# Scores masked by VectorE, no GpSimd arithmetic in the first layer, and only TensorE in source order

## The chip, the core and the metric

The kernel runs on one core of a Trainium2 chip. The metric is device time in microseconds (us) of one execution. The engines named here are TensorE (PE; its weight loads are PEld), VectorE (DVE), ScalarE (ACT), GpSimd (POOL) and SyncE (SP), whose queue issues most of the transfers. Each engine runs its own instructions in the order in which the program gives them.

## What is computed

```python
# gated linear attention: 4 sequences, 8 heads, 768 steps, head dimension 48
for t in range(S):
    state = alpha[:, :, t, :, None] * state + np.einsum('bhd,bhe->bhde', k[:, :, t], v[:, :, t])
    y[:, :, t] = np.einsum('bhd,bhde->bhe', q[:, :, t], state)
# first layer: 3072 tokens of 384, 2048 hidden; g = max(h, 0) squared
h = x @ w_in
r = np.maximum(h, 0.0)
x = (r * r) @ w_out
# second layer: each token goes to one of 8 experts of 1024 hidden
logits = x @ w_gate + modality_bias[modality_id]
e_idx = np.argmax(logits, axis=1)
out[mask] = gate_w[mask, None] * (np.maximum(x[mask] @ w1[e], 0.0) @ w2[e])
```

Inputs w_in and w_out arrive as 64-bit numbers; the kernel turns them into 32-bit ones itself.

## The kernel before

The 3072 tokens are 24 attention units of 128 tokens (unit u) and 12 blocks of 256 tokens (block n, two units each). For a unit, `a_scan` and `a_scan2` make running products of alpha (VectorE's scans, lines 319 and 331) and multiply k and q by them (lines 320 and 332: on VectorE for units 0 and 1, on GpSimd after that, by `MULD`). `a_p` makes the 128x128 scores (line 341); ScalarE copies them out of PSUM (line 348) and GpSimd sets those on the wrong side of the diagonal to zero (line 349). `a_y` multiplies them with v (lines 389 and 392), ScalarE copies y (line 394), and y goes to memory (line 397; issued from ScalarE's queue for units below `PRE` = 4, from SP's after that). `a_state` adds the unit to the running state (line 377). `a_yload` reads a block's x back (line 401) and `a_x` splits it into a high and a low part, xh and xl (lines 407 and 408).

Every product of the layers is made as three matmuls of such parts (`mm3`, line 430). A block's first layer is 16 steps; step (n, f) makes h for 128 hidden columns (tile ph), then g = max(h, 0) squared (ScalarE's line 981 and VectorE's line 985), its parts gh (ScalarE, line 989) and gl (line 991: VectorE, or GpSimd for block 1, by `POOLGL`), and three steps later adds to the output (tile po). Blocks 0 and 1 run interleaved, block 1 eight steps behind, while the weights are made ready. For each of the 16 weight blocks f, `convert(f)` decodes two halves (mag on ScalarE, line 275; three integer operations on VectorE, lines 278 to 280) and splits them (wh on ScalarE, line 258; wl on GpSimd, line 259). `gate_flip` transposes the second half (line 298, copied by line 300), and `gate_columns` appends eight columns to it (lines 305 to 307; line 307 is VectorE's). Tile st holds four loaded pieces, and the next load is issued when a piece is used up.

`put` places attention units, routing and the checks of alpha's range (`a_check`) at steps of the first layer. From step g0+9 of the last block the second layer's first weights are loaded and split (`m_load`, `m_w`). The block `with tc.manual_schedule(engines={...})` names the engines that keep the order of the source; the instructions of other engines are put in order when the program is built, by when it reckons their operands ready.

Of the kernel before, what the change touches and what calls it, by code (L numbers as in the profile page):

```python
# [8 lines left out]
F32 = mybir.dt.float32  # L9
F32R = mybir.dt.float32r  # L10
BF16 = mybir.dt.bfloat16
I32 = mybir.dt.int32
AF = mybir.ActivationFunctionType
ALU = mybir.AluOpType
# [9 lines left out]
C = 128  # L24
NU = N // C
CPB = S // C
HP = H // 2
HR = 112
TB = 256
# [150 lines left out]
def gla_moe_moe2(ctx: ExitStack, tc: tile.TileContext, ain, vin, al_d, wio_d, wg_d, wgt_d, mid_d, mb_d, w12_d, out):  # L180
    nc = tc.nc
    pe, act, dve, pool, sp = nc.tensor, nc.scalar, nc.vector, nc.gpsimd, nc.sync

    def mkpool(name, bufs=1, **kw):
        return stack.enter_context(tc.tile_pool(name=name, bufs=bufs, **kw))

    stack = ctx
    const = mkpool("const")
# [4 lines left out]
    p1 = mkpool("p1", 1)  # L193
# [10 lines left out]
    yt_d = dram.tile([DM, N], F32, name="yt_d")  # L204

    ident = const.tile([128, 128], F32, name="ident")
    tri = const.tile([128, 128], BF16, name="tri")
    ones = const.tile([128, 128], BF16, name="ones")
    iota = const.tile([128, NCOL], F32, name="iota")
    tok1 = const.tile([128, NU], F32, name="tok1")  # L210
# [44 lines left out]
    def split(t, lo_eng=dve):  # L255
        hi = wpool.tile([128, 2 * DM + E], F32R, name="wh")
        lo = wpool.tile([128, 2 * DM + E], F32R, name="wl")
        act.copy(out=hi[:, 0:2 * DM], in_=t)  # L258
        lo_eng.tensor_tensor(out=lo[:, 0:2 * DM], in0=t, in1=hi[:, 0:2 * DM], op=ALU.subtract)  # L259
        return (hi[:, 0:DM], lo[:, 0:DM]), (hi[:, DM:], lo[:, DM:])  # L260

    wreg = {}

    def load_w(f):
        for k in range(2):
            stage(("w", f, k), wio_d[f, :, DM * k:DM * (k + 1)].bitcast(I32))

    def convert(f):

        w = rows_p.tile([128, 2 * DM], I32, tag="row", name="w")  # L270
        for k in range(2):
            raw = wst.pop(("w", f, k)).bitcast(I32).rearrange("p (n two) -> p n two", two=2)
            half = w[:, DM * k:DM * (k + 1)]
            mag = p3.tile([128, DM], F32, name="mag")
            act.activation(out=mag, in_=raw[:, :, 1].bitcast(F32), func=AF.Copy, scale=2.0 ** -112)
            yield
            m = mag.bitcast(I32)
            dve.tensor_scalar(out=half, in0=m, scalar1=-(2 ** 31), scalar2=None, op0=ALU.bitwise_and)
            dve.scalar_tensor_tensor(out=half, in0=raw[:, :, 0], scalar=29, in1=half, op0=ALU.logical_shift_right, op1=ALU.bitwise_or)
            dve.scalar_tensor_tensor(out=half, in0=m, scalar=3, in1=half, op0=ALU.logical_shift_left, op1=ALU.bitwise_or)  # L280
            if k and f + 2 < NF:
                load_w(f + 2)
            yield
        w = w.bitcast(F32)
        wreg["w", f] = split(w, pool)
        gates.append((w[:, DM:], *wreg["w", f][1]))
        yield

# [24 lines left out]
    def a_scan(u):  # L313
# [3 lines left out]
        ar = ar3.rearrange("p g t -> p (g t)")  # L317
        mul = dve if u < MULD else pool
        dve.tensor_tensor_scan(out=ar, data0=al[:, 0:HP * (C + 1)], data1=delta.rearrange("p g t -> p (g t)"), initial=0.0, op0=ALU.mult, op1=ALU.add)  # L319
# [16 lines left out]
    def a_p(u):  # L336
        x = un[u]
        pp = [ps1.tile([128, HP, C], F32, tag=t, name="pp") if u in ATG else ps2.tile([128, HP, C], F32, tag="out" if u == 1 else "P", name="pp") for t in ("ms", "y")]
        for hp in range(HP):
            for j, (r0, r1) in enumerate(((0, 64), (64, HR))):  # L340
                pe.matmul(out=pp[j][:, hp, :], lhsT=x["k"][r0:r1, hp * C:(hp + 1) * C], rhs=x["q"][r0:r1, (HP - 1 - hp) * C:(HP - hp) * C], start=True, stop=True)
        x["pt"] = []
        for j in range(2):
            if u in (1, 3):
                pt = p3.tile([128, 2, XW], F32, tag="ob", name="pt").rearrange("p j d -> p (j d)")[:, 0:HP * C].rearrange("p (g t) -> p g t", g=HP)
            else:
                pt = p1.tile([128, HP, C], F32, tag=f"pt{j}", name="pt")
            act.copy(out=pt, in_=pp[j])  # L348
            pool.affine_select(out=pt, in_=pt, compare_op=ALU.is_ge, fill=0.0, base=-127, pattern=[[0, HP], [1, 128]], channel_multiplier=1)  # L349
            x["pt"].append(pt)  # L350

    def a_kt(u):
# [28 lines left out]
    def a_y(u):  # L381
        x = un[u]
        c = u // 2 % CPB

        py = ps1.tile([HR, HP, C], F32, tag="y", name="py")
        if c:
            for hp in range(HP):
                for r0, r1 in ((0, 64), (64, HR)):
                    pe.matmul(out=py[r0:r1, hp, :], lhsT=st_t[u % 2][r0:r1, hp, 0:r1 - r0], rhs=x["q"][r0:r1, (HP - 1 - hp) * C:(HP - hp) * C], start=not hp, stop=False, skip_group_check=True)
        for hp in range(HP):  # L390
            for j, (r0, r1) in enumerate(((0, 64), (64, HR))):
                pe.matmul(out=py[r0:r1, hp, :], lhsT=x["v"][:, hp, r0:r1], rhs=x["pt"][j][:, hp, :], start=not c and not hp, stop=True, skip_group_check=True)
        y = p1.tile([HR, HP, C], F32, name="y")
        act.copy(out=y, in_=py)
        yd = yt_d.rearrange("(g j e) t -> j e g t", g=HP, j=2)
        for j, (r0, r1) in enumerate(HRNG):
            (act if u < PRE else sp).dma_start(out=yd[j, :, :, u * C:(u + 1) * C], in_=y[r0:r1])

    def a_yload(n):
        x = p1.tile([128, ND, TB], F32, name="xf")  # L400
        (act if n < 2 else sp).dma_start(out=x, in_=yt_d.rearrange("(d p) t -> p d t", p=128)[:, :, n * TB:(n + 1) * TB])
        xt[n] = x

    def a_x(n):
# [27 lines left out]
    def layer1(w, x):  # L432
        ph = ps2.tile([128, TB], F32, tag="h", name="ph")
        for d in range(ND):
            mm3(ph, w, x, (slice(None), slice(d * 128, (d + 1) * 128)), (slice(None), d), d == 0, d == ND - 1)
        return ph
# [336 lines left out]
    PRE = 4  # L773
    LEAD = 8
    LAG1 = 3
    POOLGL = (1,)
    WARM = 4
    MULD = 2

    ATG = {4: 12, 5: 18, 6: 24}  # L780
    gq = {}
# [1 line left out]
    if True:  # L783
# [15 lines left out]
        def keep_warm(n):  # L799
            warm = ps2.tile([HR, HP * C], F32, tag="h", name="warm")  # L800
            for _ in range(n):
                pe.matmul(out=warm, lhsT=delta[:, 0, 0:HR], rhs=delta.rearrange("p g t -> p (g t)")[:, 0:HP * C], start=True, stop=True)
        keep_warm(WARM)
        pool.memset(ones, 1.0)
        pool.affine_select(out=tri, in_=ones, compare_op=ALU.is_ge, fill=0.0, base=-1, pattern=[[1, 128]], channel_multiplier=-1)
        pool.memset(cum, 0.0)
# [121 lines left out]
        for n in range(2, NB):  # L928
            g0 = two + (n - 2) * NF
            for i in range(2):  # L930
                u = 2 * n + 3 + i
# [35 lines left out]

            spread([g0 + k for k in (2, 5, 7)], check())

        with tc.manual_schedule(engines={mybir.EngineType.PE, mybir.EngineType.Activation, mybir.EngineType.DVE, mybir.EngineType.Pool}):  # L970
            early()
            for gs in range(len(seq) + LAG1):
                n, f = seq[gs] if gs < len(seq) else (NB, 0)
                for step in at.get(gs, ()):
                    step()
                gate = None
                alone = gs < LEAD
                if n < NB:
                    ph = layer1(wreg["w", f][0], xt[n])
                    g = p3.tile([128, TB], F32, name="g")  # L980
                    act.activation(out=g, in_=ph, func=AF.Relu)  # L981
                    if n == 0:
                        cv(f + 1)
                        gate = gate_flip()
                    dve.scalar_tensor_tensor(out=g, in0=ph, scalar=0.0, in1=g, op0=ALU.max, op1=ALU.mult)  # L985
                    if n == 0:
                        cv(f + 2)
                    gh = gpool.tile([128, TB], F32R, name="gh")
                    act.copy(out=gh, in_=g)  # L989
                    gl = gpool.tile([128, TB], F32R, name="gl")  # L990
                    (pool if n in POOLGL else dve).tensor_tensor(out=gl, in0=g, in1=gh, op=ALU.subtract)  # L991
                    gq[n, f] = (gh, gl)
                if n == 0:
                    cv(f + 2)
                if gs >= LAG1:
                    moe1_l2(*seq[gs - LAG1])
                if n == 0 and alone:
                    cv(f + 2)
                if gate:
                    gate_columns(*gate)  # L1000
                if n == 0 and alone:
                    cv(f + 3)
                if n == 1 and gs < two:
                    cv(f + LEAD + 2)
                    cv(f + LEAD + 3)
# [111 lines left out]
```

## Time and profile before

| | |
|---|---|
| median of 3 runs | 861.3 us (860.91 to 862.28) |
| the profiled execution | 860.75 us, its span 859.0 us |
| TensorE matmuls busy | 787.2 us (92%) |
| VectorE busy | 536.0 us (62%) |
| ScalarE busy | 418.5 us (49%) |
| GpSimd busy | 192.0 us (22%) |

Busy time is the time in which an engine runs an instruction, its waiting inside one included. The granted clock is TensorE's: 1.00 is 2.4 GHz and 0.50 is 1.2 GHz, and a value between them is a mean over a stretch.

### The profile page before, as it was taken

The numbers are of one execution on the slowest core, as the hardware profiler recorded it, in microseconds if no ns is written. First come the engines' busy times: TensorE is split into PE (matmuls) and PEld (weight loads), VectorE is DVE, ScalarE is ACT, GpSimd is POOL, SyncE is SP. The second block draws the span as 40 slices with busy tenths as digits, with TensorE's granted clock in tenths as the row PEclk, the third lists the DMA queues.
The fourth block names the chain that finished last, engine by engine and source line by source line (L and its number), as shares of the span: only waits on it lengthen the run. The fifth ranks groups of instructions, "written<-read, shape, count | busy, mean of one in ns | idle before, by whom it ended". The sixth has DMA issues, their size and how long they took to land. (4 is left out here: it accounts for less than half of the span.)

```text
span 859.0 us, 16686 instructions
## 1 busy us (share of the span) xinstructions
PE 787.2 (92%) x6174; PEld 752.1 (88%) x6174; DVE 536.0 (62%) x1278; ACT 418.5 (49%) x911; POOL 192.0 (22%) x206
## 2 busy tenths in 40 slices
PE   6477697999999999999999999997999999999992
PEld 4366697999999999999999999997998999999992
DVE  7577977665656565656565656456787666666631
ACT  2344453434444445545454454442666666666641
POOL 4232453442111111111111111001112232223110
PEclk9568877999999999999999999999999999999997
DMA  9646434304121323232323210102688777777600
GB/s 261 168 126 170 122 93 127 108 30 121 54 83 55 93 69 104 73 101 79 95 82 97 64 45 25 33 17 73 208 244 275 235 227 222 224 229 226 207 30 17
DMA packets 56021, 105.40 MB, mean 123 GB/s; under 512 B 9163, under 2 KB 29141, under 8 KB 55920
## 3 DMA queue, kind: packets, MB, share of 16 engines
q1 hardware_dynamic: 50256, 92.92, 36.9%
q0 software_dynamic: 3200, 9.65, 3.4%
q10 hardware_dynamic: 2464, 1.57, 0.6%
q8 instruction: 53, 0.87, 0.5%
q14 instruction: 48, 0.39, 0.1%
HBM read 89.95 MB, written 14.36 MB: 121 GB/s over the span
## 5 line engine op out<-in xcount | busy, mean ns | idle before, releaser
L430 PE MATMUL ph<-xh,wh 128*128 128x256 f32 x864 | 251.0, 291 | 8.0 <-DVE g L985 5.2
L430 PE MATMUL ph<-xh,wl 128*128 128x256 f32 x864 | 244.9, 283 | 1.8 <-POOL wl L259 1.8
L430 PE MATMUL ph<-xl,wh 128*128 128x256 f32 x864 | 245.4, 284 | 0.4 <-DVE xl L408 0.4
L430 PE MATMUL po<-wh,gh 128*128 128x392 f32 (+1 forms) x584 | 203.9, 349 | 4.2 <-ACT ob L870 2.9
L430 PE MATMUL po<-wl,gh 128*128 128x392 f32 (+1 forms) x584 | 200.0, 342 | 0.0
L430 PE MATMUL po<-wh,gl 128*128 128x392 f32 (+1 forms) x584 | 199.9, 342 | 0.0
L430 PEld LDWEIGHTS ph<-xh,wh 128*128 128x128 f32 x864 | 165.0, 191 | 11.4 <-DVE g L985 5.9
L430 PEld LDWEIGHTS ph<-xh,wl 128*128 128x128 f32 x864 | 165.0, 191 | 2.6 <-POOL wl L259 2.6
L430 PEld LDWEIGHTS ph<-xl,wh 128*128 128x128 f32 x864 | 165.2, 191 | 1.8 <-DVE xl L408 0.7
L989 ACT CAST gh<-g 128x256 fp32r<-128x256 f32 x192 | 78.0, 406 | 144.2 <-DVE g L985 144.1
L985 DVE SCALAR_TENSOR_TENSOR g<-ph,g 128x256 f32<-128x256 f32 x192 | 79.8, 416 | 95.0 <-ACT g L981 94.8
L259 DVE TENSOR_TENSOR wl<-st,wh 128x768 fp32r<-128x768 f32 x104 | 99.4, 956 | 61.4 <-ACT wh L258 60.6
L991 DVE TENSOR_TENSOR gl<-g,gh 128x256 fp32r<-128x256 f32 x176 | 82.0, 466 | 76.5 <-ACT gh L989 76.0
L430 PEld LDWEIGHTS po<-wh,gh 128*128 128x128 f32 x584 | 111.6, 191 | 7.0 <-ACT ob L870 4.6
L258 ACT CAST wh<-st 128x768 fp32r<-128x768 f32 x104 | 86.6, 834 | 60.6 <-PE po L430 40.1
L981 ACT ACTIVATE g<-ph 128x256 f32<-128x256 f32 x192 | 73.2, 381 | 87.5 <-PE ph L430 82.9
L430 PEld LDWEIGHTS po<-wl,gh 128*128 128x128 f32 x584 | 111.6, 191 | 0.0
L430 PEld LDWEIGHTS po<-wh,gl 128*128 128x128 f32 x584 | 111.2, 190 | 0.0
L320 POOL TENSOR_TENSOR qk<-qk,ar 112x512 f32<-112x512 f32 x22 | 26.8, 1218 | 160.7 <-DVE ar L319 160.3
L349 POOL TENSOR_SCALAR_AFFINE_SELECT pt<-pt 128x512 f32<-128x512 f32 x48 | 32.9, 709 | 97.1 <-ACT pt L348 97.0
L745 POOL DMA_INDIRECT out_dram<-xs,ix x25 | 25.8, 1030 | 113.6 <-ACT xs L744 57.3
L727 ACT ACTIVATE gh<-ph 128x256 fp32r<-128x256 f32 x96 | 36.9, 385 | 21.7 <-PE ph L430 19.9
(187 smaller groups left out, 913.9 us busy)
## 6 DMA issues: line engine op xcount, KB each, us to landing
st<-in_w_dram SPq DMA_DIRECT2D x104, 384.0 KB, 3.7
st<-in_wio_dram SPq DMA_DIRECT2D x32, 384.0 KB, 3.1
qk<-in_ain_dram SPq DMA_DIRECT2D x23, 448.0 KB, 4.0
al<-in_ain_dram SPq DMA_DIRECT2D x24, 226.2 KB, 2.7
v<-in_vin_dram SPq DMA_DIRECT2D x24, 224.0 KB, 3.1
scr<-ob SPq DMA_DIRECT2D x12, 385.0 KB, 2.9
st<-in_al_dram SPq DMA_DIRECT2D x12, 384.0 KB, 3.2
yt_d<-y SPq DMA_DIRECT2D x40, 96.0 KB, 2.7
```

Of the source, the lines that this page charges most:

```text
L258: act.copy(out=hi[:, 0:2 * DM], in_=t)
L259: lo_eng.tensor_tensor(out=lo[:, 0:2 * DM], in0=t, in1=hi[:, 0:2 * DM], op=ALU.subtract)
L320: mul.tensor_tensor(out=k.rearrange("p (g t) -> p g t", g=HP), in0=k.rearrange("p (g t) -> p g t", g=HP), in1=ar3[:, :, 0:C], op=ALU.mult)
L349: pool.affine_select(out=pt, in_=pt, compare_op=ALU.is_ge, fill=0.0, base=-127, pattern=[[0, HP], [1, 128]], channel_multiplier=1)
L430: pe.matmul(out=out_, lhsT=lhs[a][lsl], rhs=rhs[b][rsl], start=first and i == 0, stop=last and i == 2)
L727: act.activation(out=gh[:, cols], in_=h, func=AF.Relu)
L745: pool.indirect_dma_start(out=out[:, :], out_offset=bass.IndirectOffsetOnAxis(ap=x["ix"][:, 2 + j:3 + j], axis=0), in_=xo[:, 0:DM], in_off ...
L981: act.activation(out=g, in_=ph, func=AF.Relu)
L985: dve.scalar_tensor_tensor(out=g, in0=ph, scalar=0.0, in1=g, op0=ALU.max, op1=ALU.mult)
L989: act.copy(out=gh, in_=g)
L991: (pool if n in POOLGL else dve).tensor_tensor(out=gl, in0=g, in1=gh, op=ALU.subtract)
```

## The change

Only TensorE keeps the order of the source; VectorE, ScalarE and GpSimd are put in order when the program is built, as SP was before. A constant tile `mask` of 128x128 integers (-1 or 0) is made by GpSimd at the start, and one VectorE instruction reads the scores from PSUM, masks them with a bitwise and, and writes them. The multiplications of k and q, wl and gl are VectorE's throughout. In blocks 0 and 1 ScalarE squares g. All transfers of y and x go through SP's queue.

```diff
+    mask = const.tile([128, C], I32, name="mask")
...
-        wreg["w", f] = split(w, pool)
+        wreg["w", f] = split(w)
...
-            act.copy(out=pt, in_=pp[j])
-            pool.affine_select(out=pt, in_=pt, compare_op=ALU.is_ge, fill=0.0, base=-127, pattern=[[0, HP], [1, 128]], channel_multiplier=1)
+            dve.tensor_tensor(out=pt.bitcast(I32), in0=pp[j].bitcast(I32), in1=mask[:, None, :].to_broadcast([128, HP, C]), op=ALU.bitwise_and)
...
-            (act if u < PRE else sp).dma_start(out=yd[j, :, :, u * C:(u + 1) * C], in_=y[r0:r1])
+            sp.dma_start(out=yd[j, :, :, u * C:(u + 1) * C], in_=y[r0:r1])
...
-        (act if n < 2 else sp).dma_start(out=x, in_=yt_d.rearrange("(d p) t -> p d t", p=128)[:, :, n * TB:(n + 1) * TB])
+        sp.dma_start(out=x, in_=yt_d.rearrange("(d p) t -> p d t", p=128)[:, :, n * TB:(n + 1) * TB])
...
-    POOLGL = (1,)
+    POOLGL = ()
...
-    MULD = 2
+    MULD = NU
...
+        mkf = p1.tile([128, C], F32, tag="wt", name="mkf")
+        pool.memset(mkf, -1.0)
+        pool.affine_select(out=mkf, in_=mkf, compare_op=ALU.is_ge, fill=0.0, base=-127, pattern=[[1, C]], channel_multiplier=1)
+        pool.tensor_copy(out=mask, in_=mkf)
...
-        with tc.manual_schedule(engines={mybir.EngineType.PE, mybir.EngineType.Activation, mybir.EngineType.DVE, mybir.EngineType.Pool}):
+        with tc.manual_schedule(engines={mybir.EngineType.PE}):
...
-                    dve.scalar_tensor_tensor(out=g, in0=ph, scalar=0.0, in1=g, op0=ALU.max, op1=ALU.mult)
+                    if n < 2:
+                        act.activation(out=g, in_=g, func=AF.Square)
+                    else:
+                        dve.scalar_tensor_tensor(out=g, in0=ph, scalar=0.0, in1=g, op0=ALU.max, op1=ALU.mult)
```

TensorE's own order is the same in both programs up to the end of the first layer's steps. The line numbers of the changed kernel are up to ten higher than those of the kernel before.

VectorE near the start, before: from the end of unit 1's scans to the first decoded weights (state is the running state, w the decoded weights, ar and af the running products).

```order
L331 SCALAR_TENSOR_TENSOR af<-al,d_103 112x517
L332 TENSOR_TENSOR qk<-qk,af 112x512
L379 COPY state_104<-kv 112x4x48
L319 SCALAR_TENSOR_TENSOR ar<-al,delta 112x516
L324 TENSOR_SCALAR d_103<-ar 112x4
L325 RECIPROCAL d_103<-d_103 112x4
L331 SCALAR_TENSOR_TENSOR af<-al,d_103 112x517
L278 TENSOR_SCALAR w<-mag 128x384
```

The same place in the changed program, from the masked scores of unit 0 (pt, two halves) on:

```order
L349 TENSOR_TENSOR pt<-pp,mask 128x512 x2
L320 SCALAR_TENSOR_TENSOR ar<-al,delta 112x516
L476 COPY cm<-cum 128x8
L325 TENSOR_SCALAR d_104<-ar 112x4
L326 RECIPROCAL d_104<-d_104 112x4
L332 SCALAR_TENSOR_TENSOR af<-al,d_104 112x517
L379 COPY state_105<-kv 112x4x48
L279 TENSOR_SCALAR w<-mag 128x384
L364 TENSOR_TENSOR state_105<-state_105,ar 112x4x48
L280 SCALAR_TENSOR_TENSOR w<-st,w 128x384
L279 TENSOR_SCALAR w<-mag 128x384
L349 TENSOR_TENSOR pt<-pp,mask 128x512 x2
```

The scores come to VectorE behind both units' scans, the copy of the state moves behind the next unit's scans, and the decode is no longer done half by half.

SP's queue, changed, where the third weight block is loaded (st is a weight piece, yt_d and xf are the write of y and the read of x; before, the writes and reads of this place were on ScalarE's queue):

```order
L253 DMA st<-in_wio_dram 128x768 x2
L397 DMA yt_d<-y 48x4x128 x2
L230 DMA al<-in_ain_dram 112x517
L236 DMA qk<-in_ain_dram 112x1024
L401 DMA xf<-yt_d 128x3x256
L242 DMA v<-in_vin_dram 128x448
L253 DMA st<-in_wio_dram 128x768 x4
```

The write of unit 1's y and the read of block 0's x now stand ahead of the next four weight loads.

ScalarE where the second layer's first weights are split (wh<-st), before:

```order
L981 ACTIVATE g<-ph 128x256
L989 CAST gh<-g 128x256
L258 CAST wh<-st 128x768
L981 ACTIVATE g<-ph 128x256
L989 CAST gh<-g 128x256
L258 CAST wh<-st 128x768
```

The same place in the changed program:

```order
L985 ACTIVATE g<-ph 128x256
L996 CAST gh<-g 128x256
L985 ACTIVATE g<-ph 128x256
L996 CAST gh<-g 128x256
L259 CAST wh<-st 128x768 x2
L985 ACTIVATE g<-ph 128x256
L259 CAST wh<-st 128x768
```

The first such split has 185 instructions of the form g<-ph ahead of it before and 188 now.

## Rows read from the trace of the kernel before

**Rows 1.** Stretch, us; PE, PEld, DVE, ACT, POOL busy; clock, DMA share, GB/s

```profile
0.00:156.40 156.40, 112.53 (x773) 97.74 (x774) 118.75 (x196) 65.11 (x145) 57.83 (x59) 0.78 0.55 152
156.40:596.00 439.60, 435.63 (x3717) 418.73 (x3717) 254.79 (x746) 201.69 (x484) 74.82 (x86) 1.00 0.24 69
596.00:601.50 5.50, 0.43 (x4) 0.11 (x2) 3.12 (x17) 1.19 (x3) 2.36 (x6) 0.95 0.77 227
601.50:838.00 236.50, 233.56 (x1653) 231.11 (x1654) 157.13 (x312) 147.94 (x272) 55.06 (x56) 0.99 0.69 211
...
107.70:116.00 8.30, 8.29 (x33) 8.30 (x34) 5.26 (x10) 3.40 (x8) 2.74 (x2) 0.50 0.33 95
```

**Rows 2.** TensorE's waits, 0 to 156.4 us: us in total, times, longest

```profile
PE pwt L298 <- DVE w L280: 10.0, 2, 5.1
PE pwt L305 <- ACT wt L300: 9.1, 7, 5.7
PE pwt L298 <- DVE wl L307: 7.5, 6, 2.2
PE py L389 <- DVE wl L307: 5.7, 2, 3.0
```

**Rows 3.** VectorE's groups, 0 to 156.4 us: busy, mean ns, idle before

```profile
L280 DVE SCALAR_TENSOR_TENSOR w<-mag,w 128x384 int32<-128x384 int32 x32 | 31.6, 987 | 1.1
L278 DVE TENSOR_SCALAR w<-mag 128x384 int32<-128x384 int32 x32 | 24.7, 772 | 3.2 <-ACT mag L275 3.1
L279 DVE SCALAR_TENSOR_TENSOR w<-st,w 128x384 int32<-128x384 int32 x32 | 22.6, 708 | 1.1
L319 DVE TENSOR_TENSOR_SCAN ar<-al,delta 112x516 f32<-112x516 f32 x7 | 9.0, 1285 | 1.9 <-DMA al<-in_ain_dram 1.9
L985 DVE SCALAR_TENSOR_TENSOR g<-ph,g 128x256 f32<-128x256 f32 x21 | 8.6, 412 | 9.5 <-ACT g L981 9.5
L320 DVE TENSOR_TENSOR qk<-qk,ar 112x512 f32<-112x512 f32 x2 | 1.4, 692 | 0.4 <-DMA qk<-in_ain_dram 0.4
```

**Rows 4.** VectorE in order of time: start us, us, what

```profile
65.65 2.07 DVE L280 SCALAR_TENSOR_TENSOR w<-mag,w 128x384 int32<-128x384 int32 x1
67.64 0.41 DVE L991 TENSOR_TENSOR gl<-g,gh 128x256 fp32r<-128x256 f32 x1
67.98 0.34 DVE L278 TENSOR_SCALAR w<-mag 128x384 int32<-128x384 int32 x1
68.36 0.56 DVE L279 SCALAR_TENSOR_TENSOR w<-st,w 128x384 int32<-128x384 int32 x1
68.95 0.56 DVE L280 SCALAR_TENSOR_TENSOR w<-mag,w 128x384 int32<-128x384 int32 x1
```

**Rows 5.** GpSimd in order of time, same place

```profile
65.11 2.20 POOL L259 TENSOR_TENSOR wl<-w,wh 128x768 fp32r<-128x768 f32 x1 [2.02 <-ACT wh L258]
```

**Rows 6.** The split on VectorE, mostly in the second layer, from the page

```profile
L259 DVE TENSOR_TENSOR wl<-st,wh 128x768 fp32r<-128x768 f32 x104 | 99.4, 956 | 61.4 <-ACT wh L258 60.6
```

**Rows 7.** VectorE's waits, 0 to 156.4 us

```profile
DVE state L377 <- PE kv L374: 11.0, 3, 4.8
DVE g L985 <- ACT g L981: 9.5, 6, 2.6
DVE xl L408 <- ACT xh L407: 4.0, 1, 4.0
```

**Rows 8.** A wait of ScalarE's, 0 to 160 us

```profile
ACT mag L275 <- DMA yt_d<-y: 3.1, 1, 3.1
```

**Rows 9.** ScalarE in order of time, 590 to 602 us

```profile
589.79 0.41 ACT L989 CAST gh<-g 128x256 fp32r<-128x256 f32 x1 [0.49 <-DVE g L985]
...
591.91 0.41 ACT L989 CAST gh<-g 128x256 fp32r<-128x256 f32 x1 [0.49 <-DVE g L985]
599.24 0.83 ACT L258 CAST wh<-st 128x768 fp32r<-128x768 f32 x1 [6.92 <-DMA st<-in_w_dram]
```

**Rows 10.** Loads of w_in and w_out: count, KB, us from issue to landing

```profile
st<-in_wio_dram SPq DMA_DIRECT2D x32, 384.0 KB, 3.1
```

## The prediction

> **What bounds the kernel now.** I read the stretches first [rows 1]. From 156.4 to 596 us TensorE is busy for 435.63 of 439.60 us at a granted clock of 1.00, and from 601.5 to 838 us for 233.56 of 236.50: there is nothing to win there but by less TensorE work, and the change takes none away. The first 156.4 us are another matter. TensorE is busy for 112.53 us of them at a clock of 0.78, that is 112.53 x 0.78 = 88 us of work at the upper level of the clock (2.4 GHz); VectorE is busy for 118.75 us. This stretch ends where the sixteenth and last weight block's gate columns are made (line 305), so it is the stretch in which w_in and w_out are decoded and split, blocks 0 and 1 run, and attention units 0 to 6 are started. The third place is the short stretch from 596 to 601.5 us, where TensorE does 0.43 us of work.
>
> Next, what TensorE waits for in the first stretch [rows 2]. The four largest are 10.0 us for the decoded w (VectorE's line 280), 9.1 for the copied transposes (ScalarE), 7.5 and 5.7 for the gate columns' low part (VectorE's line 307, a 0.16 us instruction that stands behind others). VectorE, in its own fixed order, is what ends most of them.
>
> Why VectorE is late is seen in its groups and its timeline. The decode takes 32 x 3 instructions; their means are 987, 772 and 708 ns [rows 3], but undisturbed ones take 0.56, 0.34 and 0.56 us [rows 4]. The slow ones are those that meet GpSimd: the 2.07 us one starts at 65.65, while GpSimd's split of w runs from 65.11 for 2.20 us [rows 5]. It ends 0.4 us after GpSimd does. So 32 x (0.987-0.56) + 32 x (0.772-0.34) + 32 x (0.708-0.56) = 13.7 + 13.8 + 4.7 = 32 us of VectorE's busy time is waiting inside instructions.
>
> **The change, part by part, up to the sixteenth gate columns.** I counted VectorE's instructions ahead of that point in program order: 199 before, 236 after.
>
> - GpSimd does no arithmetic any more in the first layer: -32 us of stretch.
> - The mask and square of g leave VectorE: 21 x 0.412 = -8.7 us [rows 3].
> - The low part of w comes to VectorE: 16 x 0.956 = +15.3 us, the price of the same operation in the later layer [rows 6].
> - The masked scores: VectorE has no such row. Bounds are 0.56 us (the 384-element integer forms [rows 4]) and 0.956 us (768 elements [rows 6]); it has 512 elements, as the multiplication of line 320 at 692 ns [rows 3], which I take. 12 x 0.69 = +8.3 us (6.7 to 11.5).
> - The two multiplications of an attention unit: 12 more on VectorE at 0.692 = +8.3 us. Six more gl of block 1 at 0.41 = +2.5 us.
> - Work of units 7 and 8 is pulled ahead of the point: 5 scans at 1.285 [rows 3] and 6 instructions of a few elements, which I put at 0.2 us each, +7.6 us.
>
> Sum: -40.7 + 42.0 = +1.3 us. VectorE's busy time in this stretch hardly changes; what the split of work gains in stretch it spends on new work. So the gain has to come out of VectorE's idle time, 156.4 - 118.75 = 37.7 us.
>
> Of that, 11.0 us is an addition to the state that stands at the head of VectorE's order before TensorE has made kv, 9.5 us the product g that waits for ScalarE, 4.0 us the low part of x [rows 7]. Another 3.1 us is ScalarE, stopped in its own order where it issues the read of x, which waits for y to land [rows 8]; that holds up the decode. The 9.5 us go with their instruction: the square is ScalarE's, and only gl is left. For the 11.0 + 4.0 + 3.1 = 18.1 us I take half, 9 us: the changed order puts the addition, gl and the gate columns where they were reckoned to be ready, but it is still fixed beforehand. Against that stands a new wait: the first pair of masked scores now stands behind unit 1's scans and multiplications on VectorE, where GpSimd did it at once; that is 2 x 1.285 + 2 x 0.692 = 4 us later for y of unit 0 [rows 3]. 9.5 + 9 - 4 - 1.3 = 13 us. From the other side, a VectorE without any idle time would save 37.7 - 1.3 = 36 us, and with all of its idle time kept would lose 1.3. I take 13.
>
> The second gain is at 596 us. There ScalarE's order holds the first split of the second layer's weights ahead of g: it waits 6.92 us for its transfer [rows 9], and TensorE, behind it, has nothing to do for 5.50 - 0.43 = 5.07 us of that stretch [rows 1]. In the changed order three more pairs of g and gh stand ahead of that split; two such gh in a row start 2.12 us apart [rows 9], so three steps are 6.4 us, which is nearly the wait. I count 4.5 of the 5.07 us, with 0 and 5.07 as bounds.
>
> What is moved at no cost: the eight writes of y and two reads of x in this stretch go from ScalarE's queue to SP's. ScalarE gets 21 squares (near the 0.41 us of its gh of the same size [rows 9]) and loses 12 copies of scores; its 65.11 us of 156.4 [rows 1] leave room. Six of the 24 checks of alpha, of as many elements as the 0.83 us split [rows 9], now lie ahead of the point on ScalarE and most of the rest soon after; the three steps between layer 1 and layer 2 of a group (6.4 us) hide them, and without that cover they would cost up to 0.83 us each. Behind 156.4 us VectorE gets 36 masks and 32 multiplications, 68 x 0.69 = 47 us on top of 254.79 in 439.6 us: it stays under 70% and off TensorE's path. I take 0.5 us off for it.
>
> Sum: 13 + 4.5 - 0.5 = 17 us off the profiled execution's 860.75 us (its span is 859.0, with 1.75 around it), which gives 843.75. The median of the runs is 861.3, 0.55 above it; so 861.3 - 17 = 844.
>
> **The rivals.**
>
> *VectorE's idle time nearly goes (more gain).* For it: the changed order runs the decode ahead of TensorE, so the two 5 us waits for w end. If 25 to 34 of the 36 us come out, with the 4.5 at 596: 823 to 832 us. Against it: VectorE and TensorE still hand each block's gate columns back and forth.
>
> *TensorE's clock stays low and eats it.* After the 5 us wait at 102.3 TensorE runs 8.3 us at 0.50, its lower level of 1.2 GHz [rows 1]. If what waits remain keep the clock at 0.65, 88 / 0.65 = 135 us of TensorE, and with half of its four longest waits [rows 2], 16 us, the stretch takes 151: 5 us gained, and with 0 to 4.5 at 596, 852 to 856 us. The Trainium skill ("TensorE: Matmul & The Clock Gate", HAM oscillation) says that repeated pauses throttle the array each time and that the work after them runs at half clock. By that rule several shorter waits may cost less or more than two long ones; the trace agrees as far as the long ones go. Against it: the long waits are those for w, which the new order serves early.
>
> *Slower: transfers behind y on SP's queue.* SP issues in order. In the changed program a write of y, which needs TensorE, stands ahead of weight loads at four units' y, and two reads of x, which need y landed, do too. One such hold costs a load's 3.1 us to landing [rows 10] and its decode on VectorE, 0.34 + 0.56 + 0.56 us [rows 4], 4.6 us. If all six show on TensorE's path, 27 us are lost: 844 + 27 = 871 us; it decides from the fourth hold on (4 x 4.6 is over 17). Against it: in the changed order the decode of a block stands ahead of its use by more than one block, so a late load has slack. The Trainium skill ("PSUM — Partial Sum Buffer", Engine vs sequencer instructions) calls ScalarE's, VectorE's and GpSimd's queues strict FIFO; the 11.0 us of waiting [rows 7] agree, and by it any operand that is later than the order reckoned stops all behind it, on these engines too.
>
> *No change of what it says.* If the stretch were not GpSimd's doing, the 32 us would stay, and the stretch would be longer by up to as much: 844 + 32 = 876 us. The coincidence in time [rows 4, 5] speaks against it. The Trainium skill ("SBUF — State Buffer", Who interferes with whom) says that a VectorE instruction with two SBUF inputs, or in its two-port mode, and a GpSimd instruction that reads SBUF exclude each other for the whole instruction; by that rule all 32 us go, and the rows bear it out.
>
> **How the numbers follow.** The forecast, 834 to 851 us, gets 0.58; the larger gain 0.12; the low clock 0.15; no net change (the gains and a few holds cancel) 0.05; the queue or a later operand 0.08; the last rival 0.02. A measurement of this kernel tells 0.2% (1.7 us) from no change. Faster: 0.58 + 0.12 + 0.15 = 0.85; same 0.05; slower 0.10. For 8 in 10 the range holds the forecast, all of the low clock and the upper part of the larger gain: 829 to 857 us.
>
> **What would show it.** Right: in the first 140 us GpSimd is idle after its constants; the three decode forms have means near 0.56, 0.35 and 0.56 us; the line of masked scores on VectorE has a mean near 0.7 us; VectorE's busy time up to the sixteenth gate columns is 115 to 125 us and that point is reached at 138 to 148 us; the wait of 5 us before the second layer is under 1 us; from there on TensorE is as full as before. Wrong: decode means that stay near 0.8 us; loads of st whose landing ends TensorE's or ScalarE's waits right after a write of y; a granted clock below 0.7 up to the sixteenth gate columns; new waits of TensorE after 160 us.

## The result, and the profile after

The changed kernel takes 826.8 us, median of 4 runs (825.27 to 831.36), against 861.65 us (860.91 to 862.28) for the kernel before on the same chip: a ratio of 0.9605, 95% interval 0.9564 to 0.9646. That is 34.8 us faster where 17 were forecast, and below both ranges of the prediction (834 to 851, and 829 to 857 for 8 in 10). The profiled execution took 825.27 us, its span 823.6.

The stretches of the changed kernel, beside [rows 1] (stretch and its length, then busy PE, PEld, DVE, ACT, POOL, granted clock, DMA share, GB/s). The "gate point" below is the end of the sixteenth weight block's gate columns (line 306 now), 156.4 us before (the stretch of [rows 1], 0.2 us short of the last matmul's end) and 119.5 now.

```profile
0.00:119.50 119.50, 96.60 (x775) 85.31 (x776) 107.27 (x230) 71.16 (x166) 2.89 (x20) 0.89 0.73 207
36.00:119.50 83.50, 75.00 (x627) 69.94 (x626) 75.19 (x170) 58.78 (x145) 0.00 (x0) 0.94 0.67 187
119.50:559.00 439.50, 430.80 (x3691) 414.49 (x3691) 272.76 (x797) 179.56 (x449) 0.52 (x2) 1.00 0.23 66
559.00:575.00 16.00, 11.31 (x73) 10.75 (x72) 10.65 (x38) 7.06 (x14) 5.70 (x8) 0.92 0.64 223
```

All of the gain lies ahead of the gate point: 156.4 - 119.5 = 36.9 us. Behind it the kernel takes 823.6 - 119.5 = 704.1 us, 1.5 more than the 859.0 - 156.4 = 702.6 before. VectorE was busy for 118.75 us up to that point and idle for 37.65 [rows 1]; now it is busy for 107.27 and idle for 12.23. So 11.5 us came out of its busy time and 25.4 out of its idle time. Seen from TensorE, which does the same work in the same order, 15.9 of the 36.9 us are busy time (112.53 to 96.60) and 21.0 are idle time (43.9 to 22.9). Its granted clock rose from 0.78 to 0.89: with shorter waits the same work ran faster, which is a part of the gain. From 36 us to the gate point TensorE is busy for 75.00 of 83.5 us.

TensorE's longest waits up to the gate point, beside [rows 2] (us in total, times, longest):

```profile
PE ph L430 <- ACT xh L407: 4.8, 1, 4.8
PE pwt L306 <- ACT wt L301: 3.0, 6, 0.6
PE py L392 <- DVE pt L349: 3.0, 1, 3.0
PE pwt L299 <- DVE pt L349: 2.4, 2, 1.6
PE py L389 <- DVE wl L308: 1.8, 2, 1.2
```

The 10.0 us for the decoded w are down to 0.3, and the 7.5 that the transposes waited for the gate columns' low part to 1.6. The longest single one that is left is a wait for x, which goes out to memory and back; 5.4 us are behind the masked scores, and 3.0 behind the copied transposes.

VectorE's groups in the same stretch, beside [rows 3] (busy, mean ns, idle just before them):

```profile
L281 DVE SCALAR_TENSOR_TENSOR w<-mag,w 128x384 int32<-128x384 int32 x32 | 17.4, 548 | 0.0
L280 DVE SCALAR_TENSOR_TENSOR w<-st,w 128x384 int32<-128x384 int32 x32 | 17.4, 550 | 0.0
L260 DVE TENSOR_TENSOR wl<-w,wh 128x768 fp32r<-128x768 f32 x16 | 15.2, 951 | 0.3 <-ACT wh L259 0.2
L279 DVE TENSOR_SCALAR w<-mag 128x384 int32<-128x384 int32 x32 | 10.6, 352 | 1.8 <-ACT mag L276 1.2 <-PE pwt L299 0.7
L349 DVE TENSOR_TENSOR pt<-pp,mask 128x512 int32<-128x512 int32 x12 | 7.7, 682 | 0.6 <-PE pp L342 0.6
L333 DVE TENSOR_TENSOR qk<-qk,af 112x512 f32<-112x512 f32 x8 | 5.5, 687 | 0.1
L321 DVE TENSOR_TENSOR qk<-qk,ar 112x512 f32<-112x512 f32 x8 | 5.4, 680 | 0.0
```

The prices hold almost to the nanosecond: decode 548, 550 and 352 (0.56, 0.56 and 0.34 us taken), wl 951 (956), masked scores 682 (692), multiplications 680 and 687 (692). ScalarE's 21 squares took 424 ns each.

### The profile page after: what moved, and what is told of

It is laid out like the page before. It is cut to its first block, busy times and chain, and to the rows that moved or that the text cites. A ratio compares the mean times of both kernels' runs of the same rounds, so it can differ in the third digit from the quotient of the medians.

```text
span 823.6 us, 16493 instructions
## 1 busy us (share of the span) xinstructions
PE 770.1 (94%) x6174; PEld 739.2 (90%) x6174; DVE 543.5 (66%) x1370; ACT 404.2 (49%) x895; POOL 65.7 (8%) x85
## 5 line engine op out<-in xcount | busy, mean ns | idle before, releaser
L430 PE MATMUL po<-wh,gh 128*128 128x392 f32 (+1 forms) x584 | 201.1, 344 | 5.6 <-ACT ob L874 5.6
L992 DVE SCALAR_TENSOR_TENSOR g<-ph,g 128x256 f32<-128x256 f32 x160 | 67.3, 421 | 65.5 <-ACT g L985 64.9
L727 ACT ACTIVATE gh<-ph 128x256 fp32r<-128x256 f32 x96 | 37.1, 386 | 23.9 <-PE ph L430 21.0
L729 DVE SCALAR_TENSOR_TENSOR gl<-ph,gh 128x256 fp32r<-128x256 f32 x96 | 40.0, 416 | 8.2 <-ACT gh L727 8.2
L745 POOL DMA_INDIRECT out_dram<-xs,ix x25 | 27.8, 1114 | 111.9 <-ACT xs L744 56.2
```

The costliest lines, as they stand in the source:

```text
L430: pe.matmul(out=out_, lhsT=lhs[a][lsl], rhs=rhs[b][rsl], start=first and i == 0, stop=last and i == 2)
L727: act.activation(out=gh[:, cols], in_=h, func=AF.Relu)
L729: dve.scalar_tensor_tensor(out=gl[:, cols], in0=h, scalar=0.0, in1=gh[:, cols], op0=ALU.max, op1=ALU.subtract)
L745: pool.indirect_dma_start(out=out[:, :], out_offset=bass.IndirectOffsetOnAxis(ap=x["ix"][:, 2 + j:3 + j], axis=0), in_=xo[:, 0:DM], in_off ...
```

## The experiments

Each was run in three rounds beside the kernel before, whose median on the five occasions was 860.9 to 864.9 us; so a difference of a few us between two runs of different occasions is not settled where their intervals overlap. The last three columns are of the profiled execution, which can lie some us from the median: "busy" and "idle" are VectorE's up to the gate point, and "behind" is the span less that point.

| run | us | ratio (95%) | gate point | busy / idle | behind |
|---|---|---|---|---|---|
| before | 861.65 | 1 | 156.4 | 118.8 / 37.7 | 702.6 |
| changed | 826.82 | 0.9605 (0.9564–0.9646) | 119.5 | 107.3 / 12.2 | 704.1 |
| order_only | 871.13 | 1.0109 (1.0072–1.0145) | 139.7 | 114.0 / 25.7 | 728.9 |
| work_only | 858.56 | 0.9937 (0.9905–0.9969) | 149.9 | 107.1 / 42.8 | 709.5 |
| order_split_and_mul | 837.03 | 0.9654 (0.9596–0.9712) | 126.5 | 107.5 / 19.0 | 710.6 |
| vectore_free | 836.94 | 0.9688 (0.9666–0.9709) | 132.0 | 112.7 / 19.3 | 703.5 |
| scalare_free | 855.77 | 0.9900 (0.9875–0.9925) | 144.4 | 106.6 / 37.8 | 709.7 |
| split_on_gpsimd | 842.25 | 0.9753 (0.9717–0.9789) | 133.4 | 116.0 / 17.4 | 707.5 |
| mul_on_gpsimd | 850.73 | 0.9869 (0.9819–0.9919) | 130.3 | 112.6 / 17.7 | 719.4 |
| square_back_on_vectore | 830.32 | 0.9639 (0.9598–0.9679) | 121.7 | 110.3 / 11.4 | 704.6 |
| y_on_scalare_queue | 833.46 | 0.9666 (0.9623–0.9710) | 129.7 | 108.9 / 20.8 | 704.1 |
| mask_on_gpsimd | 833.43 | 0.9685 (0.9634–0.9735) | 121.8 | 106.7 / 15.1 | 706.2 |
| early_x_two_later | 823.75 | 0.9538 (0.9508–0.9568) | 120.4 | 107.2 / 13.2 | 703.8 |
| fixed_from_block_2 | 828.19 | 0.9579 (0.9521–0.9638) | 121.2 | 106.9 / 14.3 | 705.1 |
| fixed_from_block_2_late_x | 825.79 | 0.9561 (0.9521–0.9601) | 118.0 | 106.6 / 11.4 | 706.3 |
| scalar_fixed_from_2 | 826.25 | 0.9567 (0.9525–0.9610) | 120.3 | 107.9 / 12.4 | 705.1 |

### The order and the work, each alone

order_only is the kernel before with one line changed; work_only is the changed kernel with that line put back.

```diff
-        with tc.manual_schedule(engines={mybir.EngineType.PE, mybir.EngineType.Activation, mybir.EngineType.DVE, mybir.EngineType.Pool}):
+        with tc.manual_schedule(engines={mybir.EngineType.PE})
```

> The kernel before, with only TensorE in source order and nothing else changed: GpSimd still masks, multiplies and splits. Theory A (the fixed order cost VectorE its idle time, and this is the larger part): the decode means stay at 0.7 to 1.0 us, VectorE's idle time up to the sixteenth gate columns falls from 37.7 to about 13 us, and these come at 130 to 135 us; 836 to 842 us in all. Theory B (GpSimd's blocking of VectorE is the larger part): the order alone gains under 8 us, 854 us or more. Rival C (each alone gains little, since the other still holds TensorE): 850 to 858 us here and with the order kept as well.

> The changed kernel with VectorE, ScalarE and GpSimd in source order again; the moved work stays moved. Theory A: the decode means fall to 0.35 and 0.55 us and VectorE's busy time to 100 to 108 us, but its idle time stays near 37 us; sixteenth gate columns at 140 to 146 us, 846 to 852 us in all. Theory B: 830 to 838 us. Rival C: 850 to 858 us.

For the total, the reading by which each part alone gains little (C) comes nearest, though neither 871.1 nor 858.6 us lies in its 850 to 858: order_only is slower than the kernel before, which only B's "854 or more" allows. But up to the gate point order_only gains 16.7 us and work_only 6.5, which is 23 of the 37 that both gain together; and behind it order_only loses 26.3 and work_only 6.9. In work_only VectorE's busy time is that of the changed kernel (107.1) and the decode forms take 558, 558 and 353 ns in the old order: the stretch inside instructions was GpSimd's doing and is gone. Yet VectorE's idle time grew to 42.8 us. VectorE's and ScalarE's waits in work_only, 0 to 150.4 us:

```profile
DVE wl L260 <- ACT wh L259: 14.3, 12, 3.3
DVE state L377 <- PE kv L374: 11.5, 3, 4.8
DVE gl L998 <- ACT gh L996: 6.1, 4, 3.1
...
ACT g L985 <- PE ph L430: 24.3, 21, 3.2
...
ACT y L394 <- PE py L392: 16.9, 5, 5.8
ACT wh L259 <- DVE w L281: 15.0, 8, 4.7
```

VectorE stands for wh of ScalarE, ScalarE for w of VectorE, 14 to 15 us each way: in a fixed order the work that moved to VectorE turned stretch into waiting. Behind the gate point of order_only it is the free order that waits. From 200 to 500 us (VectorE's two waits for GpSimd, then both of TensorE's):

```profile
DVE af L331 <- POOL qk L332: 24.2, 11, 3.0
...
DVE ar L319 <- POOL qk L320: 7.0, 2, 5.4
...
PE po L430 <- ACT ob L870: 10.3, 5, 2.4
PE ph L430 <- DVE g L985: 10.0, 13, 2.0
```

VectorE's scans, placed early, stand behind GpSimd's multiplications, and g queues behind them. TensorE is busy for 279.7 of these 300 us, 297.7 in the kernel before.

### Which parts the order needs

order_split_and_mul is order_only with two parts of the work.

```diff
-        wreg["w", f] = split(w, pool)
+        wreg["w", f] = split(w)
...
-    MULD = 2
+    MULD = NU
```

> The kernel before with the free order and two of the parts of the new work: the split of w on VectorE and all attention multiplications on VectorE. The masks stay with ScalarE and GpSimd, gl of block 1 with GpSimd, the square with VectorE, y with ScalarE's queue. Theory (the free order lost its 16 us again because VectorE's order stood behind GpSimd in these two parts; the other parts act singly, and cost 3.5, 6.6 and 6.6 us when undone one by one in the changed kernel): 826.8 + 16.7 = 843 us, 838 to 849, the sixteenth gate columns at 125 to 135 us and less than 710 us behind them. Rival (the parts need each other: only all of them together let the order run): 852 us or more.

837.0 us, 1 us under the theory's range: with these two the free order gains 34 us over order_only, and by the medians it stands 10 us above the changed kernel (4 us by the ratios, whose intervals overlap). So the free order needs these two parts. The others together bring 10 us at most; that this is less than the 16.7 us that three of them cost one by one (gl of block 1 was never undone alone) is within the noise. The loss behind the gate point fell from 26.3 to 8.0 us.

### Whose fixed order made the idle time

The changed kernel, with one of the two engines free beside TensorE's source order.

```diff
-        with tc.manual_schedule(engines={mybir.EngineType.PE}):
+        with tc.manual_schedule(engines={mybir.EngineType.PE, mybir.EngineType.Activation, mybir.EngineType.Pool}):
```

> The changed kernel with VectorE's order free and TensorE, ScalarE and GpSimd in source order; with all four in source order it took 858.6 us, with VectorE and ScalarE free 826.8. Theory of the prediction (the idle time is VectorE's own fixed order): most of the 32 us comes, 827 to 838 us, the sixteenth gate columns at 120 to 130 us. Rival (the two engines wait for each other in their fixed orders, so freeing one leaves it waiting for the other, which is still fixed): 840 to 858 us, the point at 135 to 150 us, with ScalarE's waits for g and y still near 24 and 17 us.

(scalare_free has `DVE` in the place of `Activation`.)

> The changed kernel with ScalarE's order free and TensorE, VectorE and GpSimd in source order. Theory of the prediction (VectorE's fixed order makes the idle time): little comes, 850 to 859 us, VectorE's waits for the state and for wh stay at 11 and 14 us. Rival (half of it is ScalarE's order): 835 to 850 us and VectorE's wait for wh falls under 5 us.

Of the 31.7 us between work_only (858.6) and the changed kernel, VectorE's order alone brings 21.6, ScalarE's alone 2.8, which cannot be told from nothing (the intervals overlap), and the last 7 need both. VectorE's waits up to the gate point, vectore_free, then two of ScalarE's up to 132 us:

```profile
DVE gl L998 <- ACT gh L996: 5.0, 9, 1.2
DVE pt L349 <- PE pp L342: 3.2, 3, 1.4
DVE wl L260 <- ACT wh L259: 2.6, 4, 1.0
...
DVE state L377 <- PE kv L374: 2.3, 3, 1.3
...
ACT g L985 <- PE ph L430: 22.5, 20, 4.3
...
ACT y L394 <- PE py L392: 14.1, 5, 4.9
```

The 14.3 us for wh fell to 2.6 and the 11.5 for the state to 2.3, though ScalarE's order was that of work_only. ScalarE's own waits at g and y stayed near, 22.5 and 14.1 us, as the rival had it, and yet the gate point came 18 us earlier. In scalare_free VectorE's waits for wh and the state are 8.6 and 9.0 us, between the theory's and the rival's. The prediction was right that it was mostly VectorE's order; that the engines hold each other is true of the last quarter.

### The parts undone one by one

Each is the changed kernel with one part as before: the split of w on GpSimd (`split(w, pool)`), the multiplications there (`MULD = 2`), the square on VectorE (`if n < 0`), the transfers of y and x on ScalarE's queue, or the scores copied by ScalarE and masked by GpSimd.

> The changed kernel with the low part of w in the first layer made by GpSimd again (16 of 2 us). Theory A: VectorE loses 15.3 us of work and gets up to 16 x 1.5 = 24 us of blocking, a net of at most 9 us: 827 to 836 us. Theory B (the split was what blocked most): 838 us or more, with decode means near 0.8 us. If GpSimd hardly blocks when the order is free, the time falls below 824 us.

15.4 us slower. VectorE's decode in it:

```profile
L280 DVE SCALAR_TENSOR_TENSOR w<-st,w 128x384 int32<-128x384 int32 x32 | 19.9, 637 | 0.0
L281 DVE SCALAR_TENSOR_TENSOR w<-mag,w 128x384 int32<-128x384 int32 x32 | 19.7, 624 | 0.1
L279 DVE TENSOR_SCALAR w<-mag 128x384 int32<-128x384 int32 x32 | 14.2, 464 | 4.7 <-PE pwt L299 2.9 <-POOL wl L260 1.7
```

The time is theory B's (838 or more), its sign is not: the decode means are not near 0.8 us. A smaller stretch is back, 8.8 us on the decode (32 x 87, 76 and 112 ns), and also on the multiplications (1057 ns at line 321): VectorE is busy 8.7 us longer though 15.2 us of wl left it. By the prediction's terms this part is worth 32 - 15.3 = 16.7 us; that the 15.4 us come near it is chance, since 8.8 and not 32 us of the decode's stretch came back.

> The changed kernel (826.8 us) with the two multiplications of an attention unit on GpSimd again from unit 2 on. Theory (in the run with the free order alone, which lost 26 us behind the sixteenth gate columns, VectorE's reckoned order stands behind GpSimd's multiplications): the loss comes back here with the work of the change in place, 10 to 25 us behind the gate columns and some 3 to 6 us ahead of them by stretch, 838 to 855 us, and VectorE's waits of 200 to 500 us are ended by qk from GpSimd. Rival (that loss came of something else in the old work: the masks on GpSimd, gl on GpSimd, the decode that ran late): VectorE has 2 x 0.69 us less per unit and the time stays within 3 us, 824 to 830 us.

23.9 us slower by the medians; in the profiled executions 10.8 us ahead of the gate point, where 3 to 6 were expected, and 15.3 behind it. The theory holds. VectorE's waits from 120 to 600 us show it:

```profile
DVE af L332 <- POOL qk L333: 17.3, 11, 3.4
```

In the kernel before, the same multiplications lay on GpSimd, and no such wait is among VectorE's four from 200 to 500 us.

> The changed kernel with g of blocks 0 and 1 squared and masked by VectorE again. Theory (up to the sixteenth gate columns VectorE, busy for 107 of 119.5 us, sets the pace): 21 more instructions at 0.33 to 0.41 us, 7 to 9 us, nearly all of it on the time, 833 to 836 us, and the point moves to 126 to 128 us. Rival (TensorE and its chain with ScalarE set the pace, VectorE's 12 us of idle time take it up): 825 to 829 us, the point within 2 us of 119.5.

3.5 us slower with overlapping intervals, the gate point 2.2 later, VectorE 3.0 us busier: between the theory's 7 to 9 us and the rival's nothing. The 21 products g are 21 x 0.418 = 8.8 us more of VectorE, but one scan of each kind and one multiplication by each, 3.8 us, now lie behind the point: the free order gives way where it can.

> The changed kernel with the writes of y of units 0 to 3 and the reads of x of blocks 0 and 1 on ScalarE's queue again. Theory (ScalarE stops where it issues a read that waits for y to land; 3.1 us of that in the kernel before): 2 to 8 us slower, 829 to 835 us, with a wait on y's transfer ahead of a ScalarE instruction in the first 120 us. Rival (SP's queue is the one that holds the weight loads, so moving y off it frees it): 1 to 4 us faster, 822 to 826 us.

6.6 us slower, as the theory had it; the rival (moving y off SP's queue gains) is out, though its effect is there: ScalarE's waits for loaded pieces fall from 5.9 to 2.6 us. ScalarE stands where it issues a read behind y's landing. This wait and the one for x itself, neither of them among ScalarE's waits in the changed kernel, in its rows up to 125 us:

```profile
ACT xh L407 <- DMA xf<-yt_d: 4.6, 2, 3.8
...
ACT g L985 <- DMA yt_d<-y: 3.3, 1, 3.3
```

> The changed kernel with the scores copied by ScalarE and masked by GpSimd again. Theory (VectorE sets the pace at the start): 12 x 0.68 = 8 us leave VectorE ahead of the sixteenth gate columns, 4 to 8 us of it are gained unless GpSimd's masks stretch VectorE's work by as much; 820 to 826 us. Rival (the masked scores are on TensorE's chain: a copy, a semaphore and a GpSimd operation in the place of one VectorE instruction): TensorE's waits for pt grow from 5.4 us, and the time is 3 to 10 us longer, 830 to 837 us.

6.6 us slower: 2.3 at the gate point and 2.1 behind it in the profiled run. VectorE's busy time there is all but unchanged (106.7), since other work moved up. TensorE's wait for the masked scores up to 125 us, and the stretch up to the gate point:

```profile
PE py L393 <- POOL pt L350: 5.0, 4, 1.9
0.00:121.80 121.80, 99.42 (x775) 87.14 (x776) 106.72 (x221) 75.74 (x176) 19.71 (x32) 0.86 0.70 202
```

The rival's time came, but not its sign: with another 0.5 us at the transposes TensorE waits 5.5 us for pt, and it was 5.4 in the changed kernel. TensorE's idle time up to the point did not grow either (22.4 us, against 22.9); its busy time did, by 2.8 us, at a clock of 0.86 in the place of 0.89. So the theory's gain did not come, and why the time is longer is open.

### Behind the gate point

At the start of the second layer the old stall changed its place. TensorE in order of time, changed kernel (start, us, what, idle before it):

```profile
571.21 0.55 PE L414 MATMUL px<-ident,xs 128*128 128x128 f32 x3 [4.08 <-DMA xs<-scr,ix]
572.37 0.90 PE L414 MATMUL px<-ident,xs 128*128 128x128 f32 x3 [0.61 <-DMA xs<-scr,ix]
```

ScalarE's first split of the weights starts at 566.12 without a wait, as predicted, but TensorE's own fixed order now reaches the transposes of the gathered tokens before they have landed: 4.7 us, where 5.07 had been [rows 1]. early_x_two_later puts these transposes two steps later:

```diff
-        put(g0 + 13, lambda: m_x(EARLY[0]))
+        put(g0 + 15, lambda: m_x(EARLY[0]))
```

> The changed kernel with the transposes of the second layer's first tokens put two steps (2 x 2.1 us) later on TensorE. If the stall at the second layer's start moved from the weights to the gathered tokens, TensorE's wait of 4.1 and 0.6 us for them goes to under 0.6 us and the total falls by 3.5 to 4.5 us, to 822 to 824 us. Rival: the same wait comes back at the first step that needs these tokens, or for gathers behind them, and the total stays within 1.5 us of 826.8.

The wait is gone and 823.75 us is the lowest median of all; the gain over the changed kernel is 3.1 us by the medians, with intervals that just overlap. A new wait of 2.6 us for gh beside that place took part of it.

The last three go back to a fixed order from block 2 on: all four engines, the same with the later transposes, and TensorE and ScalarE alone with them.

```diff
+        def steps(a, b):
+            for gs in range(a, b):
...
+        with tc.manual_schedule(engines={mybir.EngineType.PE}):
+            early()
+            steps(0, two)
+        with tc.manual_schedule(engines={mybir.EngineType.PE, mybir.EngineType.Activation, mybir.EngineType.DVE, mybir.EngineType.Pool}):
+            steps(two, len(seq) + LAG1)
```

> The changed kernel up to the end of block 1 (free order, only TensorE in source order), and from block 2 on all four engines in source order again. Theory (the free order pays at the start alone; later it makes TensorE wait for ob and gather tokens early, and the fixed order of the kernel before was fuller there, 49.67 of each 50 us against 47 to 49): TensorE gets 4 to 5 us back between 200 and 500 us and the 4.7 us wait for gathered tokens goes, but the wait of about 5 us for the first split of the second layer's weights comes back, 819 to 824 us. Rival (the later loss comes from the work, the masks and multiplications on VectorE, as the fixed order with the new work was also slower there): 825 to 831 us.

> The same with the first expert slot's gathered tokens transposed two steps later in source order. Theory (the gathered tokens' wait was the free order's own; in the fixed order that place is behind the 5 us wait for weights anyway): within 2 us of the kernel without this shift. Rival (the wait for gathered tokens is there in both orders): 3 to 5 us faster than it.

> The changed kernel with TensorE and ScalarE, but neither VectorE nor GpSimd, in source order from block 2 on, and the gathered tokens transposed two steps later. Theory (TensorE's 5.6 us of waits for ob are ScalarE's freed order): those waits fall to about 2.9 us as in the kernel before, the wait for ScalarE's first split of the second layer's weights comes back with about 5 us, so 822 to 827 us. Rival (ob is late because VectorE's order makes ScalarE late): the waits for ob stay near 5.6 us and the time is 826 to 831 us.

828.2, 825.8 and 826.3 us: none can be told from the changed kernel. TensorE's waits behind 119.5 us, fixed_from_block_2, then one of scalar_fixed_from_2:

```profile
PE ph L430 <- DVE g L991: 4.6, 1, 4.6
PE po L430 <- ACT ob L874: 2.9, 9, 0.3
...
PE po L430 <- ACT ob L874: 5.5, 6, 1.1
```

The middle is fuller (295.5 of 300 us from 200 to 500, against 292.2 in the changed kernel), and the wait behind ScalarE's weights split is back with 4.6 us (g stands behind it): a trade. The waits for ob are 2.9 us where VectorE is fixed and 5.5 to 5.7 where it is free, ScalarE's order being fixed in both (scalar_fixed_from_2, vectore_free); so they go with VectorE's order, as the rival said. The later transposes brought 2.4 us by the medians with overlapping intervals, which is not settled; no wait for gathered tokens of that length stands in either.

## Why the prediction was wrong, step by step

**The place was right.** TensorE could win only in the first stretch, and all of the gain is there. The forecast for it was 13.2 us (taken as 13) and 36.9 came. Of the missing 23.7 us 12.8 lie in VectorE's busy time and 10.9 in its idle time: both terms failed.

**The stretch was right.** The decode took 32 x (987 + 772 + 708) = 78.9 us [rows 3] and takes 32 x (548 + 550 + 352) = 46.4, so 32.5 us are gone; 32 were forecast. work_only shows that this is GpSimd's absence and not the order. The new work's prices held too (above).

**The first step that failed: VectorE's busy time, forecast at +1.3 us, is -11.5.** Two things were missed. By counts and means over all groups the durations add up to 125.8 us before and 123.2 after, -2.6 instead of +1.3, a miss of 3.9 us; four scans were pulled ahead instead of five, and a scan took 1.22 to 1.23 us. And the union is smaller than the sum: 125.8 - 118.75 = 7.1 us of overlap before, 123.2 - 107.27 = 16.0 after, a miss of 8.9 us. VectorE in order of time in the changed kernel:

```profile
60.80 0.55 DVE L280 SCALAR_TENSOR_TENSOR w<-st,w 128x384 int32<-128x384 int32 x1
61.27 0.95 DVE L260 TENSOR_TENSOR wl<-w,wh 128x768 fp32r<-128x768 f32 x1
62.14 0.55 DVE L281 SCALAR_TENSOR_TENSOR w<-mag,w 128x384 int32<-128x384 int32 x1
62.61 0.55 DVE L280 SCALAR_TENSOR_TENSOR w<-st,w 128x384 int32<-128x384 int32 x1
```

Each starts 0.08 us before its predecessor ends, and none reads what that one writes (a half goes through lines 279, 280 and 281 in turn, and line 260 reads a block whose halves are both done). In [rows 4] the decode of one half stands in a chain, the second instruction at 68.36 and the third, which reads its result, at 68.95: 0.59 us apart, no overlap. The free order sets independent work between them. order_only overlaps by 13.7 us, work_only by 8.3: it is the order that does it. In such an order a sum of durations prices most instructions some 0.08 us too high. The Trainium skill ("Perfetto Trace Analysis", Optimizing Scalar/DVE Operations) says that the profiled latency holds about twice the data-access overhead, since the write half overlaps with the next instruction; the rows agree, and show that a dependent next instruction has no such overlap.

**The second step that failed: VectorE's idle time, "I take half, 9 us".** Of 37.7 us the forecast took 9.5 + 9 - 4 = 14.5 out, and 25.4 came out. The working priced the named waits one by one [rows 7, 8] and halved three of them; but vectore_free shows that an engine free to fill a wait with decode that is ready loses nearly all of the longest ones at once (14.3 to 2.6 and 11.5 to 2.3 us). The time lies in the range of the rival with more gain, 823 to 832 us, at a chance of 0.12. Its reading, that most of the idle time goes, was the better one; that its number was hit is in part luck. It counted on 25 to 34 us up to the gate point, where 36.9 came, 11.5 of them out of busy time that it left at +1.3, and on 4.5 us at 596, where 0.4 came. What was held against it, the block by block hand-over of the gate columns, does not hold up the decode, which now runs ahead. The last of its three operations and TensorE's last transposes of w, before (first two lines) and now:

```profile
L280 DVE SCALAR_TENSOR_TENSOR w<-mag,w x32: 557/558/2095, 18.0 to 152.8; 128x384 int32<-128x384 int32 x32
L298 PE MATMUL pwt<-ident,w x48: 270/328/477, 22.2 to 154.3; 128*128 128x128 f32 x48
L281 DVE SCALAR_TENSOR_TENSOR w<-mag,w x32: 529/550/552, 18.6 to 108.1; 128x384 int32<-128x384 int32 x32
L299 PE MATMUL pwt<-ident,w x48: 270/273/421, 21.7 to 117.6; 128*128 128x128 f32 x48
```

The last numbers of a line are the starts of the first and the last instruction: the last decode is 9.5 us ahead of the last transposes, and was 1.5 ahead. The 4 us for the first masked pair were too many. TensorE's first product with it, before and now:

```profile
10.95 0.43 PE L392 MATMUL py<-pt,v 128*64 128x128 f32 x2 [0.99 <-POOL pt L349]
12.57 2.33 PE L392 MATMUL py<-pt,v 128*64 128x128 f32 x15 [2.97 <-DVE pt L349]
```

It starts 1.6 us later.

**The square, the multiplications, y.** The first two were priced as VectorE's time alone, -8.7 and +8.3 us, y as a share of ScalarE's 3.1. Undone one by one they cost 3.5 (within the noise), 23.9 and 6.6 us. The multiplications were entered as a cost and are the largest single part: on GpSimd they hold up VectorE's free order.

**The second layer's wait, 4.5 us, brought 0.4.** The mechanism was right for ScalarE, but the next thing to be late was not named: the gathered tokens at TensorE.

**The slower rivals.** Of transfers held behind y on SP's queue a trace can be seen: ScalarE waits 5.9 us for loaded pieces up to the gate point, none of which stands among its waits of before. But the decode runs far enough ahead, and moving y back costs 6.6 us. The clock did not stay low. Behind the gate point the forecast had a net gain of 4.5 - 0.5 = 4.0 us; 1.5 us were lost. "As full as before" was wrong there: TensorE is busy for 292.2 of the 300 us from 200 to 500, and was for 297.7. Its waits for ob, 2.9 us before and 5.6 now, are a part of that.

## What to carry to other kernels

For a freed order, look at the engine's whole idle time and not only at halves of its named waits: here two thirds of it went, because decode that was ready could fill it. Count busy time by the steps from start to start, not by the sum of durations. A fixed order that hands work between two engines can turn a saved stretch back into waiting. But free the order only together with moving off what a slower engine does inside its chain: alone it lost 9 us here (871.1 against 862.4 in the same occasion). Before counting a removed stall as won, look in the order for the next instruction of the fixed engine and what it needs.

## What was not expected of the hardware

VectorE's independent instructions overlap by about 0.08 us in the trace and dependent ones do not, which is worth 9 us of VectorE's busy time in 119.5 here. With GpSimd's split back, not only the decode forms with two inputs stretched (550 to 637 ns) but also, as in [rows 3], the one with a single input (352 to 464).
